# A fused attention and mixture-of-experts block: one matmul more in each of seven products and two fewer in each plain one, second-layer weights loaded twice by tiles, eight query tiles to a head

## The chip, the cores and the metric
One Trainium2 chip; the kernel runs on one core of it, in one launch. The metric is the device time of an execution in microseconds (us), the median of several runs.

## The reference
2048 tokens x of width D = 448. The output is the sum of x, of an attention block (16 heads of 28) and of a mixture of 8 experts, both on the normalised x. All 8 experts are chosen for each token (K = 8), so every expert runs on every token and is weighted by a softmax over its logits. Everything is float32.

```python
xn = _layernorm(x)
# attention: qkv = xn @ wqkv; 16 heads of 28; softmax(q k^T * 28**-0.5) v; @ wo
# experts, w1: 8 x 448 x 1792, w2: 8 x 1792 x 448
for e in range(8):
    h = _silu(xn @ w1[e]) @ w2[e]
    out = out + w[e] * h          # w: softmax of xn @ w_gate
return x + attention + out
```

## The kernel before
**Precision.** TensorE works in float16. Each float32 operand is split into a high and a low float16 part, and a product takes three matmuls: high by high, high by low, low by high.

**First layer.** The 1792 hidden columns of an expert go in groups of 5, 5 and 4 tiles of 128 (`GROUPS`, 24 in all), the tokens in 4 chunks of 512 (`C`). A unit (`unit`, line 1073) is one group on one chunk. D = 448 is cut into blocks of 128, 128, 128 and 64. For four of a group's tiles, two pairs, the first two blocks of D go through a seven-product scheme (Strassen-Winograd: products of sums of weight blocks with sums of x blocks, `strassen`, line 1084, 256 tokens wide, 6 matmuls each over the two pairs), and the third block and the 64 rows left over are added by `plain` (line 1098, 8 matmuls each) and `tails` (line 1111). In a group of five the fifth tile is done directly (`single`, line 1153). The sums of weights are made for each pair in `split_w1` (line 542), into buffers `wa` (seven blocks, high and low) and `wc` (third block and rest); the sums of x in `sums_of_x` (line 1173). These are split, transposed by DMA, stored in DRAM (`xd`) and loaded again for each unit (`sums_x`, line 1225, tile `xt`).

**Second layer.** `summed` (line 1295) multiplies silu's outputs (`hh`, `hl`, made by `silu`, line 1241: tanh on ScalarE, a product on VectorE, high part on ScalarE, low part on GpSimd) with the group's second-layer weights and adds the result to `acc` on VectorE. It is put between the products of the next unit (`tick`). `load_group` (line 470) loads a group's weights `r1` and `r2` whole; `scale_w2` (line 510) finds their largest absolute value with two reductions, `split_w2` (line 624) scales and splits one tile of `r2` at a time.

**Attention.** `attention` (line 1369) goes over tiles of 128 queries, four at a time (`NB`) for a head; K, Q and V of the head are loaded for each four. Scores go to a double bank (line 1420), their extreme is found on VectorE (line 1424), the exponential on ScalarE (line 1437), its high part on ScalarE (line 1445) and its low part on VectorE (line 1440); both parts are transposed by DMA (line 1458) and multiplied with V (lines 1492, 1499). After four heads the output projection follows (`project`).

**Order of work.** No order is written out by hand. Each function adds jobs with an engine, an estimated duration, a due time v, and the buffers read and written. `Plan.run` (line 103) simulates the engines when the program is built and emits, for each engine, the job with the smallest v whose inputs and buffers are there. Buffers with one tag are a ring: they are given out in the order in which they were created, and the next one waits until one is free. The order is fixed in the program then, and each engine's queue and SP's (which issues the DMAs) runs strictly in it. First-layer and second-layer work and attention are interleaved this way from about 125 us on; before, the projections of x run (`phase0`, line 655). `phase0`'s tiles are in a pool of their own, whose room attention takes when its last job is issued.

## Time and profile before

| | |
|---|---|
| median of 3 runs | 2608.8 us (2608.79 to 2611.23) |
| the profiled execution | 2610.42 us, its span 2608.6 us |
| TensorE (PE) busy | 2572.0 us, 20863 matmuls |
| VectorE (DVE) busy | 2328.2 us |
| ScalarE (ACT) busy | 2065.4 us |
| GpSimd (POOL) busy | 1370.4 us |
| DMA queue of SP | 463 MB, 83.7% of 16 engines' span |
| granted TensorE clock | 0.999 |

The span goes from the first to the last instruction of the profiled execution. PE's busy time is the union of overlapping matmuls, so a mean duration is longer than what a matmul adds to the stream. PEld is the weight load, which overlaps. SPq is SP's queue of DMA issues.

### The profile page before, as it was taken

How to read it: one execution, taken by the hardware profiler on the slowest of the kernel's cores; microseconds unless marked ns; L12 is line 12 of the kernel's file. 1: busy time of each engine (PE TensorE's matmuls, PEld its weight loads, DVE VectorE, ACT ScalarE, POOL GpSimd, SP SyncE). 2: the span in 40 equal slices, each digit the busy share in tenths (PEclk: the TensorE clock that was granted, in tenths of full speed). 3: DMA queues.
4: the chain of work that ended last, by engine and by line, in shares of the span. 5: the costliest groups of instructions: out<-in, count | busy, mean ns of one | idle time of the engine just before them, and what ended most of it. 6: DMA issues, size and time to landing. Idle time of an engine off the chain costs nothing.

```text
span 2608.6 us, 54466 instructions
## 1 busy us (share of the span) xinstructions
PE 2572.0 (99%) x20863; PEld 1612.0 (62%) x20863; DVE 2328.2 (89%) x3127; ACT 2065.4 (79%) x2993; POOL 1370.4 (53%) x1377
## 2 busy tenths in 40 slices
PE   9999999999999999999999999999999999999999
PEld 4466666666666666666665666666666666666666
DVE  9689899988998899988999899898889889998986
ACT  5578878886887888778788888888788887878874
POOL 2365545563655545456455556456455653645633
PEclk9999999999999999999999999999999999999999
DMA  9868979887898899968898888877888888997875
GB/s 264 206 153 167 185 173 189 180 174 168 171 195 172 178 175 202 182 155 178 189 182 179 166 189 187 168 177 177 174 177 190 168 172 180 187 197 162 181 157 136
DMA packets 1262757, 466.94 MB, mean 179 GB/s; under 512 B 1169440, under 2 KB 1218080, under 8 KB 1262496
## 3 DMA queue, kind: packets, MB, share of 16 engines
q1 hardware_dynamic: 1261936, 463.44, 83.7%
q8 instruction: 164, 2.69, 0.5%
q14 instruction: 97, 0.79, 0.1%
q10 hardware_dynamic: 560, 0.02, 0.0%
HBM read 160.09 MB, written 17.35 MB: 68 GB/s over the span
## 4 chain that ended last, share of the span: by engine, by line
PE 73%; DVE 14%; ACT 8%; issue 3%; DMA 3%; SPq 0%; DVEq 0%; ACTq 0%
PE banks L1311 29%; PE banks L1090 13%; PE banks L1106 10%; PE banks L1420 7%; PE banks L1162 5%; DVE mx L1424 4%; DVE pl L1440 3%; PE banks L1499 3%; PE banks L1492 2%; ACT pf L1437 2%; ACT ph L1445 2%; DMA tl<-pl 2%; DVE t L1249 2%; PE banks L1117 2%; DVE acc L1322 1%
## 5 line engine op out<-in xcount | busy, mean ns | idle before, releaser
L1311 PE MATMUL banks<-w,hr 128*128 128x448 f16 x5364 | 1083.2, 353 | 2.1 <-DVE t L1249 1.1
L1255 POOL TENSOR_TENSOR hr<-t,hr 128x512 f16<-128x512 f32 x448 | 606.7, 1368 | 576.6 <-ACT hr L1253 553.0
L1437 ACT ACTIVATE pf<-banks,mx 128x1024 f32<-128x1024 f32 x512 | 568.9, 1111 | 322.6 <-DVE mx L1424 316.9
L1311 PEld LDWEIGHTS <-hr 128*128 128x128 f16 x5364 | 516.3, 98 | 493.2 <-issue 24.0
L1440 DVE SCALAR_TENSOR_TENSOR pl<-pf,ph 128x1024 f16<-128x1024 f32 x512 | 718.2, 1404 | 57.2 <-ACT ph L1445 56.6
L1424 DVE TENSOR_REDUCE mx<-banks 128x1 f32<-128x1024 f32 x512 | 622.4, 1216 | 77.0 <-PE banks L1420 60.3
L1445 ACT ACTIVATE ph<-pf 128x1024 f16<-128x1024 f32 x512 | 539.8, 1055 | 6.2
L1090 PEld LDWEIGHTS <-wa 128*128 128x128 f16 x4032 | 392.4, 98 | 115.9 <-issue 13.7
L1106 PE MATMUL banks<-xs,wc 128*128 128x256 f16 x3072 | 395.2, 272 | 1.0 <-DVE banks L1141 0.7
L1106 PEld LDWEIGHTS <-wc 128*128 128x128 f16 x3072 | 299.3, 98 | 61.7 <-issue 5.0
L1246 ACT ACTIVATE t<-banks,the 128x512 f32<-128x512 f32 x448 | 289.8, 683 | 54.2 <-PE banks L1117 38.7
L1249 DVE SCALAR_TENSOR_TENSOR t<-t,banks 128x512 f32<-128x512 f32 x448 | 291.6, 678 | 36.7 <-ACT t L1246 35.7
L1090 PE MATMUL banks<-xt,wa 128*128 128x256 f16 x2304 | 314.4, 272 | 5.4 <-ACT banks L1131 4.7
L1420 PE MATMUL banks<-K,Q 112*128 112x512 f16 x1024 | 306.3, 380 | 2.8 <-ACT pf L1437 2.6
L1253 ACT ACTIVATE hr<-t 128x512 f16<-128x512 f32 x448 | 267.5, 627 | 18.6 <-DVE t L1249 17.9
L1322 DVE SCALAR_TENSOR_TENSOR acc<-banks,gwe,acc 128x448 f32<-128x448 f32 x383 | 254.7, 674 | 30.5 <-PE banks L1311 29.9
L1090 PE MATMUL banks<-xs,wa 128*128 128x256 f16 x1728 | 235.8, 272 | 0.4 <-DVE acc L1322 0.4
L567 POOL TENSOR_TENSOR wc<-r,wc 128x512 f16<-128x512 f32 x64 | 83.6, 1306 | 208.1 <-ACT wc L563 186.0
L634 POOL TENSOR_TENSOR w<-r,w 128x448 f16<-128x448 f32 x112 | 138.5, 1240 | 100.8 <-ACT w L631 94.7
L1162 PE MATMUL banks<-xs,wc 128*128 128x512 f16 x704 | 164.5, 379 | 1.2 <-DVE t L1249 1.2
L1420 PEld LDWEIGHTS <-Q 112*128 112x128 f16 x1024 | 94.4, 98 | 77.3 <-issue 20.8
L1499 PEld LDWEIGHTS <-th 128*128 128x128 f16 x4096 | 118.6, 96 | 13.9 <-issue 4.7
(174 smaller groups left out, 2343.0 us busy)
## 6 DMA issues: line engine op xcount, KB each, us to landing
xt<-xd SPq DMA_DIRECT2D x71, 512.0 KB
K<-qk SPq DMA_DIRECT2D x512, 56.0 KB
r<-in_B_w_dram SPq DMA_DIRECT2D x16, 1120.0 KB
V<-vs SPq DMA_DIRECT2D x64, 256.0 KB
r<-in_B_w_dram SPq DMA_DIRECT2D x16, 960.0 KB
Q<-qk SPq DMA_DIRECT2D x256, 28.0 KB
r<-in_B_w_dram SPq DMA_DIRECT2D x8, 896.0 KB
r<-in_B_w_dram SPq DMA_DIRECT2D x8, 768.0 KB
```

What stands on the lines that cost most here:

```text
L1090: nc.tensor.matmul(bank()[:, q * HC : (q + 1) * HC], w, xx, start=(start and q == 0 and i == 0), stop=True, skip_group_check=True,)
L1106: nc.tensor.matmul(bank()[:, q * HC : (q + 1) * HC], ww, xx, start=False, stop=True, skip_group_check=True,)
L1162: nc.tensor.matmul(z(), rows[:, blk, :], xx, start=(i == 0), stop=(i == NTERM - 1))
L1246: add("ACT", 686, lambda: nc.scalar.activation(t(), z(), AF.Tanh, scale=th_()[:, 0:1]), v, r=[z, (th_, 0)], w=[t])
L1249: lambda: nc.vector.scalar_tensor_tensor(t(), t(), 1.0, z(), op0=ALU.add, op1=ALU.mult),
L1255: add("POOL", 1159, lambda: nc.gpsimd.tensor_tensor(hl(), t(), hh(), ALU.subtract), v, r=[t, hh], w=[hl])
L1311: nc.tensor.matmul(y()[:, 0:D], a, wv, start=(i == 0 and u == 0), stop=(i == g - 1 and u == 2))
L1420: nc.tensor.matmul(b()[:, cs], q()[:, q0 : q0 + P], k()[:, cs], start=True, stop=True)
L1424: nc.vector.tensor_reduce(m()[:, n, j : j + 1], b(), op=ALU.min, axis=AX.X)
L1437: nc.scalar.activation(p(), s(), AF.Exp, bias=m()[:, n, j : j + 1], scale=-1.0)
L1440: nc.vector.scalar_tensor_tensor(l()[:, js], p(), P_SCALE, h()[:, js], op0=ALU.mult, op1=ALU.subtract)
L1445: add("ACT", 1060, lambda: nc.scalar.activation(h()[:, js], p(), AF.Copy, scale=P_SCALE), v, r=[p], w=[(h, j)])
```

## The change
It does these things:
- `plain` keeps the matmuls of the third block's high part with x's high part and of the 64 left over; the two with a low part (weights high by x low, weights low by x high) leave it. Each of the seven products gets one matmul more per half instead, a mixed one: a block of the third part's weights (`crossed`, four new 128x128 blocks behind the `wa` tile, or a block of `wc`) by a block of the third part of x or a sum of such blocks, scaled by `LAMBDA`.
- `split_w1` makes the four new blocks for each pair: one ScalarE copy (`less`), four GpSimd operations (`crosses`, `more_crosses`). The single tile's `wc` goes into a ring of its own, `wz`, of one buffer.
- `sums_of_x` makes the sums of the third block for each chunk on VectorE (`first_two`, `last_two`); x's sums are 6 blocks in each of two half tiles `xt` (3 buffers in place of 2 whole ones of 8 blocks), transposed, stored and loaded by halves. At the start the second half of the second chunk's sums lies in a buffer of the ring `wa`.
- second-layer weights are loaded by tiles of 128x448 into a ring of two buffers, once for the largest value (`scale_w2`, one reduction per tile) and once more for the split.
- `s5` moves into the ring `th` of silu's intermediate; `u`, `ro` and `ohl` of attention share one buffer (`uo`); `wo` in `phase0` is loaded into two buffers of the query and key weights.
- attention takes eight query tiles to a head: K and V are loaded once for eight, the output buffer `ost` holds eight.

```diff
-NB, TL, TH = 4, 1, 4
-RWA, RWC, RW2, RH, RHC, RT, RPP, RPF = 4, 4, 7, 8, 2, 3, 2, 2
+NB, NH, TL, TH = 4, 8, 1, 4
+RWA, RWC, RWZ, RW2, RH, RT, RPF, RR = 4, 4, 1, 7, 8, 3, 2, 2
+LAMBDA = 2048.0
...
+    def tile_of_w2(gi, j, name, v):
+        e, f0, _ = GROUPS[gi]
+        b = buf("mp", [P, D], F32, f"r2{name}{gi}_{j}", tag="r2", bufs=RR)
+        dma(lambda: b(), lambda: w2[e, (f0 + j) * P : (f0 + j + 1) * P, :], v, w=[b], kb=224, rate=3.6)
+        return b
...
     def scale_w2(gi, v):
...
+        for j in range(g):
+            r2 = tile_of_w2(gi, j, "m", v)
+            add("DVE", 600, lambda j=j, r2=r2: abs_max(m5()[:, j : j + 1], r2(), AX.X), v, r=[r2], w=[(m5, j)])
+        def most_of_all():
+            for i, (j0, j1) in enumerate(((0, 2), (2, g))):
+                nc.vector.tensor_reduce(m2()[:, i : i + 1], m5()[:, j0:j1], op=ALU.max, axis=AX.X)
...
-        wa = buf("mp", [P, 2, 7 * P], F16, f"wa{gi}_{j}", tag="wa", bufs=RWA)
+        wa = buf("mp", [P, 18 * P], F16, f"wa{gi}_{j}", tag="wa", bufs=RWA)
...
+        def less():
+            nc.scalar.activation(
+                r(2, 3), wc()[:, 0 : 2 * P].rearrange("p (k c) -> p k c", k=1), AF.Copy, scale=1 / LAMBDA
+            )
+        def crosses():
+            a11, a21 = r(2, 3, 0, 1)[:, 0], r(2, 3, 1, 2)[:, 0]
+            nc.gpsimd.tensor_tensor(crossed(3), a21, of_wc(1, 1), ALU.add)
+            nc.gpsimd.tensor_tensor(crossed(1), a11, a21, ALU.subtract)
+        def more_crosses():
+            a11 = r(2, 3, 0, 1)[:, 0]
+            nc.gpsimd.tensor_tensor(crossed(0), crossed(3), a11, ALU.subtract)
+            nc.gpsimd.tensor_tensor(crossed(2), of_wc(1, 0), crossed(0), ALU.subtract)
...
     def split_w2(gi, j, v):
         w = buf("mp", [P, 2, D], F16, f"w2_{gi}_{j}", tag="w2", bufs=RW2)
-        so, r2 = SC[gi][1], R[gi][1]
+        so, r2 = SC[gi][1], tile_of_w2(gi, j, "s", v)
...
-            s5 = buf("mp", [P, C], F32, f"s5{name}", tag="s5")
+            s5 = buf("mp", [P, C], F32, f"s5{name}", tag="th", bufs=RT)
...
-                        for i, (w, xx) in enumerate(((h, xp[0]), (h, xp[1]), (l, xp[0]))):
+                        for i, (w, xx) in enumerate(((h, xp[0]), (h, xp[1]), (l, xp[0]), (wx, xx3))):
...
-                        for ww, xx in (
-                            (w[:, 0, 0], xs[:, 2, t[i]]), (w[:, 0, 0], xs[:, 6, t[i]]), (w[:, 1, 0], xs[:, 2, t[i]]),
-                            (w[:, 0, 1], xs[:, 3, t[i]]),
-                        ):
+                        for ww, xx in ((w[:, 0, 0], xs[:, 2, t[i]]), (w[:, 0, 1], xs[:, 3, t[i]])):
...
+            def first_two():
+                t1, t2 = pair(0)
+                nc.vector.tensor_tensor(t1, b12, b11, ALU.subtract)
+                nc.vector.scalar_tensor_tensor(t2, t1, -LAMBDA, b22, op0=ALU.mult, op1=ALU.add)
+            def last_two():
+                t1, t2, t3, t4 = *pair(0), *pair(1)
+                nc.vector.scalar_tensor_tensor(t3, b12, -LAMBDA, b22, op0=ALU.mult, op1=ALU.add)
+                nc.vector.tensor_tensor(t4, b21, t2, ALU.subtract)
+                nc.vector.tensor_scalar(t1, t1, LAMBDA, None, op0=ALU.mult)
...
         def sums_x(gi, b, v):
-            XS_[gi, b] = x = buf("mp", [P, 8, HC], F16, f"xt{gi}_{b}", tag="xt", bufs=2)
+            first = not gi and b < 2
+            own = 3 - 2 * b if first else 2
+            xt = [buf("mp", [P, 6, HC], F16, f"xt{gi}_{b}_{q}", tag="xt", bufs=3) if q < own else None for q in range(2)]
+            XS_[gi, b] = [x or buf("mp", [P, 18 * P], F16, f"xw{b}_{q}", tag="wa", bufs=RWA) for q, x in enumerate(xt)]
...
-        TILES = [(4 * k + a, t0 + n) for k in range(H // 4) for t0 in range(0, NT, NB) for a in range(4) for n in range(NB)]
+        TILES = [(4 * k + a, t0 + n) for k in range(H // 4) for t0 in range(0, NT, NH) for a in range(4) for n in range(NH)]
...
             if i % NB == 0:
-                load_k(i, 0, at(i - 2) if i else at(-9))
-                load_k(i, 1, at(i - 1))
-                load_v(i, at(i - 2))
+                if i % NH == 0:
+                    load_k(i, 0, at(i - 2) if i else at(-9))
+                    load_k(i, 1, at(i - 1))
+                    load_v(i, at(i - 2))
```

## Rows read from the trace of the kernel before

**Rows 1.** The table of engines: busy time, share of the span, instructions.
```profile
PE 2572.0 (99%) x20863; PEld 1612.0 (62%) x20863; DVE 2328.2 (89%) x3127; ACT 2065.4 (79%) x2993; POOL 1370.4 (53%) x1377
```

**Rows 2.** Busy time of each engine in two windows: PE, PEld, DVE, ACT, POOL (with instructions), granted clock, DMA share, GB/s.
```profile
0.00:130.00 130.00, 121.84 (x592) 57.99 (x593) 103.17 (x262) 74.43 (x146) 39.66 (x50) 1.00 0.91 235
130.00:2543.00 2413.00, 2388.68 (x19727) 1514.39 (x19725) 2182.61 (x2808) 1959.74 (x2801) 1307.55 (x1303) 1.00 0.85 177
```

**Rows 3.** The waits of PE: us in total, times, longest us.
```profile
PE banks L1492 <- DMA tl<-pl: 6.5, 7, 2.1
PE banks L1090 <- ACT banks L1131: 4.7, 6, 1.3
```

**Rows 4.** PE's groups of matmuls, shapes apart: count, busy us and mean ns of one, idle time before.
```profile
L1106 PE MATMUL banks<-xs,wc 128*128 128x256 f16 x3072 | 395.2, 272 | 1.0 <-DVE banks L1141 0.7 <-DVE the L505 0.3
L1090 PE MATMUL banks<-xt,wa 128*128 128x256 f16 x2304 | 314.4, 272 | 5.4 <-ACT banks L1131 4.7 <-DVE banks L1137 0.2
L1090 PE MATMUL banks<-xs,wa 128*128 128x256 f16 x1728 | 235.8, 272 | 0.4 <-DVE acc L1322 0.4
```

**Rows 5.** The chain of waits between 1200 and 1260 us: start, us, what.
```profile
1210.56 0.87 PE banks L1106 x8
...
1221.24 0.54 PE banks L1117 x8
...
1232.98 1.31 PE banks L1090 x12
```

**Rows 6.** DVE's groups, shapes apart: count, busy us and mean ns of one, idle time before.
```profile
L1440 DVE SCALAR_TENSOR_TENSOR pl<-pf,ph 128x1024 f16<-128x1024 f32 x512 | 718.2, 1404 | 57.2 <-ACT ph L1445 56.6
...
L412 DVE TENSOR_REDUCE mb<-r 128x1 f32<-128x896 f32 x32 | 34.2, 1074 | 2.2 <-DMA r<-in_B_w_dram 2.2
L412 DVE TENSOR_REDUCE mb<-r 128x1 f32<-128x1344 f32 x16 | 24.7, 1543 | 1.2 <-DMA r<-in_B_w_dram 1.2
...
L1481 DVE TENSOR_REDUCE top<-mx 128x4 f32<-128x8 f32 x64 | 9.6, 150 | 0.2
L1183 DVE TENSOR_SCALAR xa<-acc,rstd,shift 128x256 f32<-128x256 f32 x16 | 7.3, 492 | 0.1
```

**Rows 7.** Line 412's reductions of a 128x448 and a 128x896 f32 tile, listed by line: duration ns min/median/max (the 603 is that of the 128x448 ones).
```profile
L412 DVE TENSOR_REDUCE mkq<-rqk x5: 603/1067/1068, 12.1 to 20.8; 128x1 f32<-128x896 f32 x3, 128x1 f32<-128x448 f32 x2
```

**Rows 8.** ACT's group of 128x256 copies in the split of first-layer weights.
```profile
L586 ACT ACTIVATE wa<-r 128x256 f16<-128x256 f32 x48 | 19.2, 400 | 0.0
```

**Rows 9.** The costliest and the cheapest of POOL's groups of 128x128 f32 operations on first-layer weights.
```profile
L598 POOL TENSOR_TENSOR r<-r 128x128 f32<-128x128 f32 x48 | 35.1, 732 | 3.8
...
L597 POOL TENSOR_TENSOR r<-r 128x128 f32<-128x128 f32 x48 | 24.7, 515 | 2.1
```

**Rows 10.** Line 1440 listed by line: duration ns min/median/max, first and last start.
```profile
L1440 DVE SCALAR_TENSOR_TENSOR pl<-pf,ph x512: 1205/1224/3096, 142.0 to 2572.4; 128x1024 f16<-128x1024 f32 x171
```

**Rows 11.** The DMA queue of SP (packets, MB, share of 16 engines), and issues with their sizes.
```profile
q1 hardware_dynamic: 1261936, 463.44, 83.7%
...
xt<-xd SPq DMA_DIRECT2D x71, 512.0 KB
K<-qk SPq DMA_DIRECT2D x512, 56.0 KB
...
V<-vs SPq DMA_DIRECT2D x64, 256.0 KB
```

**Rows 12.** SP's time to issue a DMA on line 388: ns min/median/max.
```profile
L388 SPq DMA_DIRECT2D K<-qk x512: 313/383/1988, 130.5 to 2531.1; - x171
...
L388 SPq DMA_DIRECT2D r<-in_B_w_dram x96: 383/526/2395, 10.6 to 2427.8; - x96
```

**Rows 13.** The timeline of PE from 124 to 138 us: start, us, line; the end of the first unit and the start of the second.
```profile
135.38 0.61 PE L1117 MATMUL banks<-xs,wc 64*128 64x256 f16 x8
...
137.03 0.82 PE L1090 MATMUL banks<-xt,wa 128*128 128x256 f16 x6
```

**Rows 14.** The timelines of PE, ACT, POOL, SP and DVE about the end of one group (1281 to 1303 us): the last second-layer products with the old weights and the first with the new, the split of two tiles between, the load of the weights of the group after, their first reduction.
```profile
1283.48 1.87 PE L1311 MATMUL banks<-w,hr 128*128 128x448 f16 x9
...
1296.66 1.31 PE L1311 MATMUL banks<-w,hr 128*128 128x448 f16 x6
...
1283.42 0.65 ACT L630 ACTIVATE r<-r,scob 128x448 f32<-128x448 f32 x1
...
1284.75 2.20 POOL L634 TENSOR_TENSOR w<-r,w 128x448 f16<-128x448 f32 x2 [0.91 <-ACT w L631]
...
1286.98 0.41 SPq L388 DMA_DIRECT2D r<-in_B_w_dram  x1
...
1295.90 1.54 DVE L412 TENSOR_REDUCE mb<-r 128x1 f32<-128x1344 f32 x1
```

**Rows 15.** The timeline of SP's queue: the transposes of the sums of chunks 2 and 3 into two `wa` buffers.
```profile
105.47 2.89 SPq L1213 DMA_TRANSPOSE xw<-xt  x1
...
124.96 1.26 SPq L1213 DMA_TRANSPOSE xw<-xt  x1
```

**Rows 16.** The timeline of PE: the first product of the fourth unit.
```profile
189.78 0.82 PE L1090 MATMUL banks<-xs,wa 128*128 128x256 f16 x6
```

**Rows 17.** The waits of DVE: us in total, times, longest us.
```profile
DVE mx L1424 <- PE banks L1420: 60.3, 70, 3.7
DVE pl L1440 <- ACT ph L1445: 56.6, 74, 2.3
```

More of the change, by code (lines that the diff above doesn't have):

```diff
@@ L618, in split_w1 @@
         add("ACT", 630, high, v, r=keys, w=[(wc, 0)])
-        add("POOL", 1303, low, v, r=[*keys, (wc, 0)], w=[(wc, 1)])
+        add("POOL", 1303, low, v, r=[*keys, *third, (wc, 0)], w=[(wc, 1)])
         add("ACT", 630, high_sums, v, r=ab, w=[(wa, 2)])
         add("POOL", 1377, low_sums, v, r=[*ab, (wa, 2)], w=[(wa, 3)])
+        add("ACT", 420, less, v, r=[(wc, 0)], w=third)
+        add("POOL", 1150, crosses, v, r=[(wc, 1), *third], w=[(wa, 4)], steps=2)
+        add("POOL", 1150, more_crosses, v, r=[(wc, 1), *third], w=[(wa, 4)], steps=2)
         W1[gi, j] = wa, wc
@@ L633, in low @@
         def low():
[L634 to L637 removed]
+            nc.gpsimd.tensor_tensor(w()[:, 1, :], r2(), w()[:, 0, :], ALU.subtract)
+        add("ACT", 1265, high, v, r=[so], w=[r2, (w, 0)])
+        add("POOL", 1038, low, v, r=[r2, (w, 0)], w=[(w, 1)])
         W2[gi, j] = w
@@ L1171, in single, with blocks, sums_of_x @@
             return lastz
-        def sums_of_x(c, x, v):
+        def blocks(b):
+            return b() if len(b.shape) == 3 else b()[:, 0 : 6 * HC].rearrange("p (k c) -> p k c", k=6)
+        def sums_of_x(c, xt, v):
+            far = [q for q in range(2) if not xt[q]]
+            xws = []
             for j in range(2):
@@ new lines, in last_two @@
+            def last_two():
[3 more added lines that the diff above has]
+                nc.vector.tensor_scalar(t1, t1, LAMBDA, None, op0=ALU.mult)
+            outs = [(xws[0], "third", q) if q in far else (xt[q], 2) for q in range(2)]
+            add("DVE", 560, first_two, v, r=xkeys(c), w=outs[:1], port=138)
+            add("DVE", 760, last_two, v, r=xkeys(c), w=outs, port=600)
@@ L1223, in sums_of_x @@
+            for q in range(2):
+                dma(
+                    lambda q=q: xd[c, q, :, 4:6],
+                    lambda q=q: xws[0]()[:, 8 * P + 2 * q * HC : 8 * P + 2 * (q + 1) * HC].rearrange("p (k c) -> p k c", k=2)
+                    if q in far else blocks(xt[q])[:, 4:6],
+                    v, r=[outs[q]], w=[("xd", c, q, 2)], kb=128,
                 )
         def sums_x(gi, b, v):
-            XS_[gi, b] = x = buf("mp", [P, 8, HC], F16, f"xt{gi}_{b}", tag="xt", bufs=2)
-            if not gi and b < 2:
-                sums_of_x(b, x, v)
+            first = not gi and b < 2
```

182 lines of the change are left out of this document (103 added, 79 removed).

## The prediction

> **What bounds the kernel now.** I read the table of engines first: TensorE (PE) is busy 2572.0 us of a span of 2608.6 us, VectorE (DVE) 2328.2, ScalarE (ACT) 2065.4, GpSimd (POOL) 1370.4 [rows 1]. Then two windows, to see where PE is not busy: 8.2 us of the first 130 and 24.3 of the 2413 in the middle, which leaves some 4 of its 36.6 idle us for the last 65, at a granted clock of 1.00, the 2.4 GHz level [rows 2]. Then PE's list of waits: its largest entries are 6.5 us over seven waits for a DMA and 4.7 over six for ACT [rows 3]. So the kernel is bound by the number of PE columns, and nothing else is a constant brake; DVE at 2182.6 of 2413 us (90%) in the middle is the next engine. Last I read the price of a matmul from the chain of waits, not from its duration: one 128x256 matmul "takes" 272 ns, but eight in a row advance the chain by 0.87 us and twelve by 1.31 us, 109 ns each [rows 4, 5].
>
> **PE work removed and added.** A unit (one chunk of 512 tokens in one group of weights; 24 groups x 4 chunks = 96 units) issues 42 matmuls in the seven products and 32 in the four plain ones; the counts 4032 and 3072 are 96 times that [rows 4]. After the change each product has one more matmul per half (+14), and each plain one keeps 2 of 4 (-16): 5376 and 1536, two fewer per unit, 192 fewer in all. Shape, type and bank halves are the same, and every matmul has its own weight load before and after. 192 x 109 ns = **21.0 us less**. If a pair went at the share of PE's busy time that falls on it, 129 to 137 ns a matmul [rows 4], it would be 26 us; I take 21, the pitch in an undisturbed row. All other PE work stays.
>
> **DVE.** The two reductions over a group's second-layer weights (34.2 + 24.7 us in all) become one per tile, 112 at 603 ns (a 128x448 reduction) = 67.5, and two tiny ones per group, 48 x 150 ns = 7.2: +15.8 us [rows 6, 7]. The sums of the third block of x are 5 operations of 128x256 for each of 4 chunks; the nearest row is the 492 ns of a 256-wide f32 one [rows 6], which makes 10 us; with operands of half the size it may be half of that, and I take the row. Together +26 us, 2354.
>
> **ACT.** One 128x256 copy per pair of weight tiles, 48 x 400 ns = +19.2 us [rows 8]: 2085 of some 2590, still 80%. It is covered: ACT's 540 us of idle time hold it. Uncovered it would be those 19 us.
>
> **POOL.** Four 128x128 operations per pair of tiles, 192; the lines that do such operations average 515 to 732 ns [rows 9]: 99 to 141 us, and I take the middle, +120. POOL is idle 1238 us, and a group's weights are split during the group before, so the time itself is hidden. What it does to DVE isn't: the subtraction on line 1440, which reads two SBUF tiles, has a median of 1224 ns and a mean of 1404 [rows 6, 10]; 512 x 180 ns = 92 us are lost beside 1370 us of POOL, 0.067 us for each. 120 x 0.067 = +8 us of DVE; bounds 0 and 120 (every microsecond blocks DVE). I take the measured share. DVE is then 2362 us.
> The Trainium skill (SBUF — State Buffer, Who interferes with whom) states that such a DVE instruction and a GpSimd one that reads SBUF exclude each other for a whole instruction; at its worst, each new POOL operation on the other's time, DVE would gain the 120 us of the upper bound. The trace agrees that they disturb each other, but shows a fifteenth of that.
>
> **DMAs and SP's queue.** K goes from 512 loads of 56 KB to 256, V from 64 of 256 KB to 32: -23 MB. The second-layer weights come twice (+25.7 MB; 24 loads become 224 tiles of 224 KB), and the sums of x as 142 loads of 384 KB in place of 71 of 512 (+18.6 MB); with 1 MB more of stores the sum is +22 MB [rows 11]. At the 235 GB/s of the first 130 us with the engines 91% busy [rows 2] that is 85 us of all engines: the queue's 83.7% becomes 87 to 88%. Issuing: -256 x 0.383 - 32 x 0.38 + 200 x 0.383 to 0.526 + 71 x 0.38, so -7 to +22 us on SP [rows 12]: 1% of its time, nothing. SP is behind in order: a load of a tile waits there until a reduction or a split frees one of two buffers, and the transposes of the probabilities queue behind it. Against that, half of the loads of K go, which wait there for the scores that free their buffers.
>
> **Buffers.** Halving the loads of K and V, the larger output buffer and the shared "uo" buffer cost PE nothing: they move only when tiles are loaded. The sum held in "th" now takes one of silu's three buffers, in turn after the last of the unit before. Usually more than 11 us lie between a unit's tails (1221.24) and the next unit's second product (1232.98) [rows 5]; at the tightest place 1.65 us do (135.38 to 137.03) [rows 13]. I price it at 0 to 5 us.
> Second-layer weights at a group's end: at 1285.3 PE ends the last product with the old ones, at 1296.66 begins the first with the new: 11.3 us, in which it does the next unit's products [rows 14]. In this time tile 2 must be split (2.4 us, from 1283.42 to half of the POOL pair), which frees the buffer for tile 4, and tile 4 must land and be split (2.4 us). A landing of up to 6.5 us is hidden; the 1.1 MB load issued at 1286.98 was being reduced at 1295.90, 8.9 us, and a fifth of the bytes should take less [rows 14]. Cost 0; at the 8.9 us it is 2.4 us at each of the 8 boundaries between groups of five, 19 us.
> At the start, the sums of chunks 2 and 3 go through one "wa" buffer in place of two, since the second chunk keeps one. A buffer turned over in 19.5 us (105.47 to 124.96) [rows 15]; four turns reach 105 + 4 x 19.5 = 183, and chunk 3 is wanted by the unit that begins at 189.8 [rows 16]. It just fits; 0 to 12 us, I take 2.
>
> **Sum.** PE is idle 24.3 us in the middle because feeders are late now and then. DVE's idle share there falls from 9.5% to about 7.6% (2182.6 + 26 in 2392 us); if late arrivals grow as that share shrinks, x 1.25, that is +6; fewer waits at K's buffers give some back: +3, and +2 at the start. 2608.6 - 21 + 5 = 2592.6 of span. The profiled execution took 2610.42, 1.8 above its span, and the median of the runs is 2608.8, 1.6 below it; so 2594.4 for such an execution and **2593 us** for the median.
>
> **Rivals.**
> (1) DVE takes over as the bound: slower. If its 280 us of idle time are waits for an order that doesn't shrink, the span is 2362 + 280 = 2642 us. It decides from the point where DVE gives up less than 33 of its 280 us. For it: DVE waits 56.6 us for ACT's copy on line 1445, which gets no faster; against it: 60.3 us are waits for PE's scores, and PE has less to do [rows 17]. Chance 0.10.
> (2) The gain is there and waits take it: tile 4 late at each boundary between groups of five (19), the start (5): 2608.8 - 21 + 24 = 2612. For it, the thin slack at a boundary (6.5 us against at most 8.9) and at the start (183 against 189.8); against it, PE has attention work to put in. Chance 0.17.
> (3) Small loads are slow ones and fill the DMA engines. The queue is busy 83.7% of the span, 2183 us; with the 85 us above, 340 us stay free. At the rate used above a tile of 229 kB takes 0.89 us of all engines [rows 2]; it decides from the point where each of the 224 takes 1.5 us more. At 2.6 us a tile the queue alone needs 2183 + 85 + 224 x 1.7 = 2650 us. Chance 0.03.
> The Trainium skill (DMA: Bandwidth & Descriptors, Measured) advises loads of 1 MiB or more, and its fit of 2.0 us plus bytes over 436 GB/s gives 2.5 us for a tile, an estimate, which would all but bring this rival about; the window's rate, reached by loads in flight together, speaks against adding up the fixed part.
> (4) The change does not do what it says: the matmuls are two fewer, but the mixed ones advance 112 ns each in place of 109, which undoes the gain (6912 x 3 ns = 21 us); 2609. Nothing in the rows speaks for it. Chance 0.03.
> The forecast keeps 0.67.
>
> **Range and chances.** A change of under 0.2%, 5.2 us, is about what a measurement of this kernel can't tell from none (three runs lie 2.4 us apart). Faster than 2603.6: nearly all of the forecast and a little of (2), 0.69; within 0.2%: most of (2), (4), the worst of the forecast, 0.15; slower: (1), (3), the rest of (2), 0.16. The low end is the 26 us of the busy shares with no new wait, 2583, rounded to 2584; the high end 2614 is where (2) ends, and leaves (1) and (3) out.
>
> **What would show it.** Right: 5376 and 1536 matmuls in the two lines, PE's busy time down by 21 us, its idle time in the middle 24 to 35 us, DVE near 2360. Wrong: PE idle over 50 us with DVE or the reduction of a tile named as releaser (1); gaps before the second-layer products at every second or third group's end, with a weight load as releaser (2); PE waiting over 20 us for the transposed probabilities (3); eight matmuls in over 0.88 us (4).

## The result and the profile after

The changed kernel takes 2624.7 us (median of four runs, 2620.7 to 2626.8); the kernel before, on the same chip, 2609.95. The ratio is 1.0053 [1.0040, 1.0066]: slower by 0.5%, where 2593 us (2584 to 2614) and a gain of 0.6% were predicted. The profiled execution took 2626.82 us with a span of 2625.0, 16.4 us above that of before.

The table of engines of the kernel after, and the DMA queue of SP (answers to [rows 1, 11]):

```profile
PE 2562.2 (98%) x20671; PEld 1595.8 (61%) x20671; DVE 2349.4 (90%) x3261; ACT 2074.7 (79%) x3041; POOL 1475.5 (56%) x1569
...
q1 hardware_dynamic: 1275888, 485.73, 87.8%
```

PE has its 192 matmuls fewer, but is busy only 9.8 us less, and idle for 62.8 us (2625.0 - 2562.2) where it was idle for 36.6. The missing 11 us of the 21 are matmuls at a lower clock: the records have 27 us at the 1.2 GHz level beside 3 before, in five stretches that each begin during or just after waits of PE of 2 to 3 us (those before 136.35, 147.89, 602.26, 911.52 and 1021.99 us). So 26.2 of idle time plus 11 of clock minus 21 of work is the 16 us. Two windows of the kernel after (columns as in [rows 2]) say where:

```profile
0.00:130.00 130.00, 123.65 (x603) 59.23 (x604) 107.44 (x280) 74.38 (x147) 44.22 (x59) 1.00 0.90 236
130.00:2543.00 2413.00, 2359.44 (x19449) 1484.77 (x19447) 2207.84 (x2927) 1974.72 (x2851) 1407.74 (x1486) 0.99 0.90 187
```

The middle is idle for 53.6 us in place of 24.3, with the DMA engines at 0.90 in place of 0.85. Its first 35 us alone, after and then before, in the same columns:

```profile
130.00:165.00 35.00, 24.00 (x141) 14.07 (x139) 25.58 (x38) 21.55 (x28) 5.74 (x5) 0.80 0.89 197
```
```profile
130.00:165.00 35.00, 33.55 (x239) 21.94 (x237) 29.69 (x43) 30.13 (x46) 23.67 (x24) 1.00 0.67 155
```

Here PE works 9.6 us less than before, and at a granted clock of 0.80. The other 20 us of idle time that the middle has gained lie behind this stretch. The timelines of ACT, DVE and PE in this stretch of the kernel after (start, us, what, idle time before it and its releaser; answers to [rows 13]):

```profile
129.63 0.60 ACT L1172 ACTIVATE s<-banks 128x512 f32<-128x512 f32 x1 [1.33 <-POOL xt L1246]
135.03 0.69 ACT L1330 ACTIVATE t<-banks,the 128x512 f32<-128x512 f32 x1 [4.80 <-DVE banks L1180]
...
131.88 0.62 DVE L413 TENSOR_REDUCE mb<-r2m 128x1 f32<-128x448 f32 x1 [4.25 <-DMA r2m<-in_B_w_dram]
...
133.16 1.03 PE L1133 MATMUL banks<-xt,wa 128*128 128x256 f16 x8 [2.60 <-DVE banks L1176]
136.35 1.01 PE L1504 MATMUL banks<-K,Q 112*128 112x512 f16 x2 [2.15 <-DMA K<-qk]
...
147.89 1.01 PE L1504 MATMUL banks<-K,Q 112*128 112x512 f16 x2 [2.94 <-ACT pf L1521]
151.19 1.44 PE L1201 MATMUL banks<-xs,wc 128*128 128x512 f16 x3 [2.29 <-DVE t L1333]
```

DVE stands 4.25 us at a reduction whose tile has not landed. The addition on line 1176, which is behind it in DVE's order, then lets PE go on at 133.16, and through line 1180 the tanh waits on ACT. One landing stops three engines, because each works in order. It isn't the only late one: the next wait of PE, before 136.35, is for a tile of K, and the chain of waits there passes over that landing:

```profile
127.85 6.94 DMA K<-qk
```

A reduction's tile is late again further on: DVE and PE about 905 us, and the chain of waits there.

```profile
902.58 0.67 DVE L1406 SCALAR_TENSOR_TENSOR acc<-banks,gwe,acc 128x448 f32<-128x448 f32 x1
907.44 0.62 DVE L413 TENSOR_REDUCE mb<-r2m 128x1 f32<-128x448 f32 x1 [4.18 <-DMA r2m<-in_B_w_dram]
...
911.52 1.01 PE L1504 MATMUL banks<-K,Q 112*128 112x512 f16 x2 [3.09 <-ACT pf L1521]
```
```profile
901.42 5.99 DMA r2m<-in_B_w_dram
```

PE's line names ACT; the chain goes back from there through two DVE operations to the reduction and its tile. The lists of waits of the kernel after, for PE, DVE and ACT (answers to [rows 3, 17]; a wait is put down to the last link only):

```profile
PE banks L1504 <- ACT pf L1521: 19.3, 21, 3.1
PE banks L1576 <- DMA tl<-pl: 6.7, 6, 3.2
PE banks L1133 <- DVE banks L1176: 4.5, 6, 2.6
...
DVE mb L413 <- DMA r2m<-in_B_w_dram: 9.6, 6, 4.3
DVE scbb L438 <- DMA scmb<-mxs: 4.0, 5, 2.1
...
ACT r2s L660 <- DMA r2s<-in_B_w_dram: 3.6, 1, 3.6
```

PE's groups of matmuls, and two pieces of its chain of waits near 1337 us (answers to [rows 4, 5]):

```profile
L1133 PE MATMUL banks<-xs,wa 128*128 128x256 f16 x1920 | 279.3, 274 | 0.0
L1145 PE MATMUL banks<-xs,wc 128*128 128x256 f16 x1536 | 225.8, 273 | 2.8 <-DVE banks L1180 1.7 <-DVE top L1565 1.1
L1395 PE MATMUL banks<-w,hr 128*128 128x448 f16 x5364 | 1083.6, 353 | 2.9 <-DVE t L1333 1.5 <-DMA Q<-qk 0.6 <-DVE u L1601 0.4
...
1337.32 0.88 PE banks L1133 x8
1338.19 0.44 PE banks L1145 x4
```

The pitch is 109 to 110 ns, mixed matmuls included, and no second-layer product waits for a split tile. Last, the new operations on POOL and ACT, and the lines of the subtraction and of the reductions with their duration in ns, min/median/max (answers to [rows 7 to 10]):

```profile
L636 POOL TENSOR_TENSOR wa<-wa,r 128x128 f16<-128x128 f16 x48 | 34.6, 720 | 0.0
L632 POOL TENSOR_TENSOR wa<-r 128x128 f16<-128x128 f32 x48 | 27.8, 579 | 0.0
L637 POOL TENSOR_TENSOR wa<-wc,wa 128x128 f16<-128x128 f16 x48 | 25.1, 522 | 3.8
L631 POOL TENSOR_TENSOR wa<-r,wc 128x128 f16<-128x128 f32 x48 | 24.8, 517 | 18.5 <-ACT r L625 18.1
...
L625 ACT ACTIVATE r<-wc 128x256 f32<-128x256 f16 x48 | 19.8, 412 | 1.6 <-POOL wc L572 1.6
...
L1524 DVE SCALAR_TENSOR_TENSOR pl<-pf,ph x512: 1205/1226/5930, 143.1 to 2542.6; 128x1024 f16<-128x1024 f32 x171
...
L413 DVE TENSOR_REDUCE mb<-r2m x112: 601/607/621, 68.3 to 2486.3; 128x1 f32<-128x448 f32 x112
```

### The profile page after: what moved, and what is told of

Same layout as the page of the kernel before. It is cut to its first block, busy times and chain, and to the rows that moved or that the text cites. A ratio compares the mean times of both kernels' runs of the same rounds, so it can differ in the third digit from the quotient of the medians.

```text
span 2625.0 us, 54530 instructions
## 1 busy us (share of the span) xinstructions
PE 2562.2 (98%) x20671; PEld 1595.8 (61%) x20671; DVE 2349.4 (90%) x3261; ACT 2074.7 (79%) x3041; POOL 1475.5 (56%) x1569
## 3 DMA queue, kind: packets, MB, share of 16 engines
q1 hardware_dynamic: 1275888, 485.73, 87.8%
## 4 chain that ended last, share of the span: by engine, by line
PE 68%; DVE 16%; ACT 7%; DMA 5%; issue 3%; POOL 1%; SPq 0%; DVEq 0%; ACTq 0%; POOLq 0%
PE banks L1395 27%; PE banks L1133 16%; PE banks L1504 6%; PE banks L1145 5%; DVE pl L1524 4%; PE banks L1201 4%; DVE mx L1508 4%; PE banks L1583 3%; ACT pf L1521 2%; PE banks L1576 2%; DVE t L1333 2%; PE banks L1156 2%; PE banks L962 1%; ACT ph L1529 1%; DVE acc L1406 1%
## 5 line engine op out<-in xcount | busy, mean ns | idle before, releaser
L1339 POOL TENSOR_TENSOR hr<-t,hr 128x512 f16<-128x512 f32 x448 | 594.6, 1341 | 584.0 <-ACT hr L1337 541.8
L1524 DVE SCALAR_TENSOR_TENSOR pl<-pf,ph 128x1024 f16<-128x1024 f32 x512 | 729.7, 1427 | 39.8 <-ACT ph L1529 37.5
L1508 DVE TENSOR_REDUCE mx<-banks 128x1 f32<-128x1024 f32 x512 | 622.8, 1216 | 62.6 <-PE banks L1504 54.6
L1133 PEld LDWEIGHTS <-wa 128*128 128x128 f16 x4800 | 468.0, 98 | 130.3 <-issue 16.7
L1133 PE MATMUL banks<-xt,wa 128*128 128x256 f16 x2866 | 384.9, 272 | 8.6 <-DVE banks L1176 4.5
L1504 PE MATMUL banks<-K,Q 112*128 112x512 f16 x1024 | 308.4, 382 | 21.8 <-ACT pf L1521 19.3
L1133 PE MATMUL banks<-xs,wa 128*128 128x256 f16 x1920 | 279.3, 274 | 0.0
L1145 PE MATMUL banks<-xs,wc 128*128 128x256 f16 x1536 | 225.8, 273 | 2.8 <-DVE banks L1180 1.7
L664 POOL TENSOR_TENSOR w<-r2s,w 128x448 f16<-128x448 f32 x112 | 136.4, 1220 | 155.4 <-ACT w L661 144.1
L1145 PEld LDWEIGHTS <-wc 128*128 128x128 f16 x1536 | 149.2, 98 | 46.4 <-issue 7.8
```

The costliest lines, as they stand in the source:

```text
L1133: nc.tensor.matmul(bank()[:, q * HC : (q + 1) * HC], w, xx, start=(start and q == 0 and i == 0), stop=True, skip_group_check=True,)
L1145: nc.tensor.matmul(bank()[:, q * HC : (q + 1) * HC], ww, xx, start=False, stop=True, skip_group_check=True,)
L1339: add("POOL", 1159, lambda: nc.gpsimd.tensor_tensor(hl(), t(), hh(), ALU.subtract), v, r=[t, hh], w=[hl])
L1504: nc.tensor.matmul(b()[:, cs], q()[:, q0 : q0 + P], k()[:, cs], start=True, stop=True)
L1508: nc.vector.tensor_reduce(m()[:, n, j : j + 1], b(), op=ALU.min, axis=AX.X)
L1524: nc.vector.scalar_tensor_tensor(l()[:, js], p(), P_SCALE, h()[:, js], op0=ALU.mult, op1=ALU.subtract)
```

## The experiments

Two kinds are to be kept apart. In e1 to e5 and e9 every engine keeps the order of the kernel that was edited; in the others the planner makes a new order. Two runs change nothing but the order: e17 that of before (+0.3%), e12 that of after (+0.6%). All ratios are to the kernel before on the same chip; "idle" is the span less PE's busy time of the profiled execution, "130 to 195" PE's busy us there and the granted clock.

| kernel | us | ratio | PE idle | DMA queue | 130 to 195 |
|---|---|---|---|---|---|
| before | 2602 to 2611 | 1 | 36.6 | 83.7% | 63.6, 1.00 |
| after | 2624.7 | 1.0053 [1.0040, 1.0066] | 62.8 | 87.8% | 54.0, 0.89 |
| e1 before, fewer matmuls | 2597.1 | 0.9965 [0.9952, 0.9978] | 41.2 | 82.5% | 63.0, 1.00 |
| e18 the same, new order | 2596.6 | 0.9971 [0.9959, 0.9983] | 38.2 | 83.0% | 62.9, 1.00 |
| e17 before, new order | 2612.7 | 1.0027 [1.0015, 1.0039] | 36.0 | 82.1% | 61.2, 0.95 |
| e4 before, load twice | 2710.0 | 1.0405 [1.0389, 1.0420] | 104.6 | 81.9% | 59.6, 0.95 |
| e10 before, eight query tiles | 2597.3 | 0.9967 [0.9953, 0.9981] | 25.0 | 78.8% | 63.2, 1.00 |
| e6 before, tiles | 2691.5 | 1.0327 [1.0312, 1.0343] | 98.1 | 89.2% | 62.9, 1.00 |
| e9 e6, small first loads | 2670.5 | 1.0248 [1.0232, 1.0264] | 87.1 | 87.0% | 62.6, 1.00 |
| e13 e6, five buffers | 2707.7 | 1.0396 [1.0380, 1.0411] | 108.3 | 89.8% | 57.6, 0.92 |
| e11 tiles and eight query tiles | 2656.1 | 1.0198 [1.0182, 1.0215] | 68.7 | 87.5% | 62.3, 1.00 |
| e2 after, memsets | 2612.5 | 1.0028 [1.0016, 1.0039] | 52.8 | 86.6% | 53.9, 0.89 |
| e3 after, small first loads | 2605.5 | 0.9997 [0.9988, 1.0007] | 45.8 | 83.2% | 56.2, 0.89 |
| e5 e2 and e3 | 2605.9 | 1.0000 [0.9990, 1.0009] | 46.8 | 83.6% | 56.6, 0.89 |
| e12 after, later landing planned | 2633.6 | 1.0109 [1.0091, 1.0127] | 63.1 | 85.2% | 52.4, 0.92 |
| e7 after, four query tiles | 2638.0 | 1.0128 [1.0114, 1.0143] | 66.9 | 88.5% | 54.1, 0.92 |
| e8 e7, own s5 | 2650.7 | 1.0173 [1.0159, 1.0187] | 77.3 | 89.5% | 56.0, 0.95 |
| e14 after, three tile buffers | 2636.0 | 1.0127 [1.0112, 1.0142] | 70.4 | 86.0% | 43.8, 0.79 |
| e15 e7, own chunk sums, six split tiles (2 runs) | 2694.9 | 1.0348 [1.0327, 1.0369] | 109.1 | 87.7% | 55.2, 0.89 |
| e16 e7, no tiles, five split tiles | 2738.1 | 1.0509 [1.0485, 1.0532] | 144.4 | 88.4% | 41.1, 0.84 |

`Plan.run` also leaves the span that it simulated when it made the order (`self.span`), a figure of the program and not of the chip. It is 2589 us for before, 2571 for after, 2583 for e6, 2584 for e11, 2580 for e13, 2591 for e17 and 2584 for e12. So after's order promises 18 us of the 21, and the order of tiles alone is 6 us shorter than before's, though it runs 85 us longer: what these kernels lose comes from work or landings that take longer than the planner assumes, not from a longer order. e15's and e16's orders, 2605 and 2600 us, are longer by themselves.

**e1: before, 192 matmuls fewer.** In the plain scheme's loop:

```diff
-                        ):
+                        )[: 3 if f and i else 4]:
```

> The kernel before, in its own order, without the last matmul of one plain product (the 64-row block's high part, in both halves): 192 matmuls of 128x256 less, nothing else changed; the output lacks that part. If PE's columns set the pace (the prediction's first term), the time falls by 21 us, to 2589, and PE's idle time stays near 37 us. If the order's other engines set the pace in places, PE's idle time grows and the time falls by less: by 10 us if half of it turns into waits, by nothing if DVE is the bound.

0.35% less, 9 us of the 21. The profiled spans, from different chips, show PE's busy time down by 17.9 and 4.6 more of idle time, 13 us; the interval of the ratio allows 6 to 12.5. So part of the removed work comes back as waiting even where nothing is added.

**e2: after, mixed blocks as memsets.**

```diff
-            nc.gpsimd.tensor_tensor(crossed(3), a21, of_wc(1, 1), ALU.add)
-            nc.gpsimd.tensor_tensor(crossed(1), a11, a21, ALU.subtract)
+            nc.gpsimd.memset(wa()[:, 14 * P : 16 * P], 0.0)
...
-            nc.gpsimd.tensor_tensor(crossed(0), crossed(3), a11, ALU.subtract)
-            nc.gpsimd.tensor_tensor(crossed(2), of_wc(1, 0), crossed(0), ALU.subtract)
+            nc.gpsimd.memset(wa()[:, 16 * P : 18 * P], 0.0)
```

> The changed kernel in its own order, with the four GpSimd operations per pair of tiles that make the mixed blocks replaced by two fills with zero (128x256 each), which read nothing; the mixed products are zero. Theory 'GpSimd blocks VectorE' (single subtractions on VectorE took up to 5.9 us beside GpSimd): POOL's busy time falls by 70 to 100 us, the mean of the subtraction on VectorE falls from 1427 to about 1390 ns, the longest ones vanish, and the time falls by 5 to 15 us. Theory 'late landings': no more than 3 us. Theory 'start': PE busy in 130 to 195 us stays at 54 of 65.

POOL's busy time falls by 80 us and the whole by 0.25%, 6.5 us. The stall at 130 us stays. But the theory that GpSimd blocks VectorE isn't shown by it: the subtraction's mean goes from 1427 to 1424 ns only, where 1390 was expected, and its longest stays at 5.9 us. By what the 6.5 us come is open.

```profile
L1520 DVE SCALAR_TENSOR_TENSOR pl<-pf,ph 128x1024 f16<-128x1024 f32 x512 | 728.4, 1424 | 35.2 <-ACT ph L1525 33.1 <-DMA tl<-pl 1.6
```

**e3: after, small first loads.** The reduction reads 64 loaded columns seven times.

```diff
-        dma(lambda: b(), lambda: w2[e, (f0 + j) * P : (f0 + j + 1) * P, :], v, ...)
+        n = 64 if name == "m" else D
+        dma(lambda: b()[:, 0:n], lambda: w2[e, (f0 + j) * P : (f0 + j + 1) * P, 0:n], v, ...)
```

> The changed kernel in its own order; the first load of each second-layer weight tile, for the largest value, brings 64 of 448 columns, and the reduction reads these 64 seven times, so VectorE works as long as before; the scale comes from a seventh of the weights. 22 MB less by DMA, and each of these loads lands sooner. Theory 'late landings' (VectorE waits in order for such a load, 9.6 us in all, and PE after it): that wait falls below 2 us, the DMA queue's share from 87.8 to about 84%, PE's idle time from 63 to 50 us or less, the time by 8 to 15 us. Theories 'GpSimd blocks VectorE' and 'start': under 4 us.

The loss is gone: 0.56%, 15 us, for 22 MB, with all operations in place. The waits of DVE for first tiles fall from 9.6 to 4.0 us (below 2 was expected), those of PE for `tl` from 6.7 to 2.4. A shorter load is both fewer bytes on the queue and an earlier landing of its own; this run doesn't part the two.

```profile
DVE mb L413 <- DMA r2m<-in_B_w_dram: 4.0, 3, 3.1
PE banks L1577 <- DMA tl<-pl: 2.4, 1, 2.4
```

**e4: before, each group's load of w2 issued twice.**

```diff
+        def twice():
+            for _ in range(2):
+                nc.sync.dma_start(r2()[:, 0:g, :], w2[e, cs, :].rearrange("(f p) d -> p f d", p=P))
```

> The kernel before in its own order, each group's second-layer weights loaded twice by the same whole load (24 more DMAs, 25.7 MB): the change's traffic without its small tiles, its two buffers and its new waits. If DMA traffic itself costs time (transposes land later): DMA share 83.7 to 88%, PE's waits for the transposed probabilities from 6.5 to over 15 us, time up by 8 us or more. If only waits for particular loads cost: time within 3 us of before.

105 us for 25.7 MB. The list of waits of DVE:

```profile
DVE mb L412 <- DMA r<-in_B_w_dram: 45.5, 14, 6.3
```

The DMA engines are not full (81.9%); the reduction, placed for one load, stands in DVE's order until both have landed. The Trainium skill (DMA: Bandwidth & Descriptors, Measured) advises loads of 1 MiB or more. No run here tests size alone: these loads of 0.9 and 1.1 MB stand in an order made for loading once, the tiles of e6 (85 us for the same bytes) in an order made for tiles.

**e5: e2 and e3 together.** Both diffs above.

> The kernel after in its own order of work, with both earlier cuts at once: the first loads of w2's tiles bring 64 of 448 columns (the reductions read those seven times), and the four mixed blocks of a pair of hidden tiles are two memsets on POOL instead of four tensor operations. It leaves out most of the maxima of w2 and the mixed blocks' values. Alone the small loads gave 0.56 % (0.9997 in place of 1.0053) and the memsets 0.25 % (1.0028). Theory A (transfers and the port shared by DVE and POOL cost separately, and the start's jam of some 10 us stays): the gains add, 0.9972 of before, about 2598 us, with the first 65 us after 130 still at 54 to 56 us of TensorE work. Theory B (both cuts take away the same late DVE operations): the gains don't add, about 0.9995, 2604 us. If the removed matmuls paid in full and nothing else was left, it would be 0.992, 2585 us.

They don't add: 1.0000 beside 0.9997, theory B in its number. Mixed blocks and late tiles don't cost separately.

**e6: before, w2 by tiles, twice.** Buffers, reductions and split as in the change's diff (`tile_of_w2`, `scale_w2`, `split_w2`), all else as before.

```diff
-        r2 = buf("mp", [P, GMAX, D], F32, f"r2_{gi}", tag="r2")
+        b = buf("mp", [P, D], F32, f"r2{name}{gi}_{j}", tag="r2", bufs=RR)
...
-        so, r2 = SC[gi][1], R[gi][1]
+        so, r2 = SC[gi][1], tile_of_w2(gi, j, "s", v)
```

> The kernel before with one part of the change alone: w2 comes by tiles of 128x448 in two buffers, once for the maxima and once for the split, in place of one load of a group; mixed products, query tiles and the chunk sums stay as before, and its order of work is planned anew. Theory A (the second load costs time by lateness): 10 to 18 us slower than before, ratio 1.004 to 1.007, with DVE's reductions waiting for tiles (some 10 us) and transposed probabilities late. Theory B (the second load is hidden where POOL's mixed blocks and the shared buffers are absent): within 0.2 % of before.

85 us, about five times the 10 to 18 that theory A expected. The waits of PE, DVE and ACT:

```profile
PE banks L1496 <- DMA tl<-pl: 29.7, 23, 3.0
PE banks L1424 <- ACT pf L1441: 14.9, 20, 2.2
...
DVE mb L412 <- DMA r2m<-in_B_w_dram: 24.7, 14, 5.2
DVE scba L437 <- DMA scma<-mxs: 4.8, 4, 1.6
DVE scbb L437 <- DMA scmb<-mxs: 4.3, 5, 1.3
...
ACT r2s L634 <- DMA r2s<-in_B_w_dram: 10.5, 5, 2.8
```

DVE and ACT stand 44 us at landings of second-layer weights and of scales (the last four lines), and PE then at what the two make: `pf`, and `pl` through its transpose.

**e9: e6's order, small first loads** (the diff of e3).

> The kernel of the run with tiles alone, in its own order of work, with the first loads of w2's tiles cut from 448 to 64 columns (the reductions read those seven times; most of the maxima are left out). Theory A (the time follows the bytes that the DMA engines have to carry: tiles alone had 492.7 MB, 89.2 % of the engines' time and 2691 us): with 470.6 MB the share falls to some 84 % and the time to 2605 to 2615 us. Theory B (not the bytes but the order: the split waits for a second landing, tiles come in two buffers, and the plan was made with shorter landings): the time stays above 2660 us with tl<-pl still ending 20 us or more of TensorE's idle time.

Some 20 us of the 85 go with the bytes of the first loads, as the 15 in e3; 65 do not: theory B, though `tl` costs PE no less than with full loads. Its waits:

```profile
PE banks L1497 <- DMA tl<-pl: 30.7, 26, 2.9
...
DVE mb L412 <- DMA r2m<-in_B_w_dram: 15.9, 9, 4.2
...
ACT r2s L635 <- DMA r2s<-in_B_w_dram: 7.3, 4, 2.8
```

**e13: e6 with five buffers for tiles.** Planned anew.

```diff
-RWA, RWC, RW2, RH, RHC, RT, RPP, RPF, RR = 4, 4, 7, 8, 2, 3, 2, 2, 2
+RWA, RWC, RW2, RH, RHC, RT, RPP, RPF, RR = 4, 4, 7, 8, 2, 3, 2, 2, 5
```

> The kernel before with w2 by tiles loaded twice (2691 us), with five buffers for the tiles in place of two, so that a tile's load needn't wait for a reduction or a split to free one; bytes are the same. Theory A (two buffers: a load stands in SP's queue until one is free, lands late, and what follows it in SP's and DVE's order is late too): the 65 us that aren't bytes mostly go, 2620 to 2640 us. Theory B (the number of separate DVE operations and landings, whatever the buffers): 2670 us or more.

Theory B: five buffers don't help. The splits no longer wait for tiles, but the waits only move to the scales:

```profile
DVE scba L437 <- DMA scma<-mxs: 20.5, 9, 4.3
DVE scbb L437 <- DMA scmb<-mxs: 17.3, 9, 4.1
...
DVE mb L412 <- DMA r2m<-in_B_w_dram: 12.8, 10, 2.2
```

**e10: before, eight query tiles.** As in the change; loads of K and V under

```diff
+                if i % NH == 0:
```

> The kernel before with another part of the change alone: eight query tiles to a head, so that K and V are loaded half as often (23 MB less); weights in one load of a group, no mixed products. Theory A (bytes are what costs beyond some 84 % of the DMA engines' time, and before stands below it): little to gain, 2597 to 2606 us, DMA share 79 to 80 %. Theory B (before too loses its 20 to 30 us of idle time to late transfers): 2585 to 2595 us.

Faster than both kernels, 0.9967, with 23 MB less (theory A, at its fast end); the waits of DVE and ACT for weights and scales are down to 0.2 us.

**e11: tiles and eight query tiles, no mixed products** (e6 and e10).

> The kernel before with two parts of the change, w2 by tiles loaded twice and eight query tiles, without the mixed products. Bytes are as before's within 4 MB. Theory A (bytes): 2605 to 2620 us, DMA share 84 to 85 %, so the 85 us of tiles alone are given back. Theory B (order and lateness of the tiles): 2660 us or more.

Bytes as before, yet 50 us slower, just short of theory B. Its engines, and what waits:

```profile
PE 2585.3 (97%) x20863; PEld 1615.0 (61%) x20863; DVE 2344.7 (88%) x3239; ACT 2064.1 (78%) x2993; POOL 1379.1 (52%) x1377
...
PE banks L1424 <- ACT pf L1441: 17.1, 22, 3.8
PE banks L1496 <- DMA tl<-pl: 14.0, 8, 2.7
...
ACT r2s L634 <- DMA r2s<-in_B_w_dram: 10.4, 6, 3.9
```

From here the kernel after differs by the mixed products and the sums of x: PE's busy time falls by 23.1 us, its idle time by 5.9, the ratio by 0.0145. That is 38 us, more than the 21 that the removed matmuls can give, so the order or the other buffers have a share in it; with 7 and 15 us for an order alone (e17, e12) the part of the matmuls can't be told from this. **What it does show: the tiles cost time in e11 already, without a mixed product.**

**e12: after, a tile planned to land 5.5 us after its issue.**

```diff
-        dma(..., kb=224, rate=3.6)
+        dma(..., kb=224, rate=3.6, land=5500)
```

> The kernel after with one number of its planner changed: a tile of w2 is taken to land 5.5 us after its issue, so that the operations that read it are given later places in the engines' orders. Nothing is computed otherwise. Theory A (DVE's reduction stands in order in front of operations that could run, so lateness turns into TensorE's idle time): the waits of the reduction on its tile (9.6 us) go below 4 us, and the time falls by 5 to 15 us, 2610 to 2620 us. Theory B (the DMA engines are full; whoever is asked later waits instead, transposes above all): the reduction's waits go, tl<-pl or pf waits of TensorE grow by as much, and the time stays within 5 us of after.

The reduction's waits on its tiles go, `pf` costs PE 30.2 in place of 19.3, and the time is 0.56% longer by the ratios: theory B in kind, at more than its price. (The profiled execution, 2623.8 us, is the fastest of the four; the others took 2633 to 2635.) The stall at the start stays, 52.4 us of work: the chain there still begins at the landing of a tile (4.83 us from 126.57) and now comes by way of POOL and a copy on ACT to the same addition on line 1176, 2 us later than in the kernel after. A later place for the reduction moves the wait and doesn't end it.

```profile
PE banks L1504 <- ACT pf L1521: 30.2, 27, 4.0
...
134.45 0.70 DVE L1176 TENSOR_TENSOR banks<-banks,s 128x512 f32<-128x512 f32 x1 [7.33 <-ACT s L1172]
```

**e7 and e8: after with four query tiles; then s5 with its own buffer.**

```diff
-NB, NH, TL, TH = 4, 8, 1, 4
+NB, NH, TL, TH = 4, 4, 1, 4
...
-            s5 = buf("mp", [P, C], F32, f"s5{name}", tag="th", bufs=RT)
+            s5 = buf("mp", [P, C], F32, f"s5{name}", tag="s5")
```

> The kernel after with four query tiles to a head in place of eight: keys and values are loaded for each four, and the outputs' buffers are half as large. It frees room, which the next kernel uses; by itself it is the base for that one. More transfers of K and V than in the kernel after, so not faster than it: 1.005 to 1.010 of before, and the stall at 130 to 160 us as after (TensorE 54 us busy of the 65 from 130 to 195, granted clock 0.89).

> The kernel of the run before this one (after, four query tiles) with one line changed back: the copy s5 of a product's bank has a buffer of its own again and doesn't take its turn among the three of the chunk sums. Theory A (s5 behind the sums of chunk 2 and 3, which wait for the one buffer of split weights, makes the stall at 130 to 160 us): the 65 us from 130 have 60 to 65 us of TensorE work at a clock near 1.00, and the time falls by 8 to 12 us against the kernel with four query tiles. Theory B (the stall is made by w2's tile loads that land late there, DVE waiting in order for them): the window stays below 57 us with a clock of 0.9, and the time falls by under 4 us.

Four tiles cost 0.75%, more than expected. An own s5 gives 2 us of work in the window and a longer whole: s5's turn in "th" is not the stall.

**e14: after, three buffers for raw tiles, six for split ones.**

```diff
-RWA, RWC, RWZ, RW2, RH, RT, RPF, RR = 4, 4, 1, 7, 8, 3, 2, 2
+RWA, RWC, RWZ, RW2, RH, RT, RPF, RR = 4, 4, 1, 6, 8, 3, 2, 3
```

> The kernel after with three buffers for the raw tiles of w2 in place of two, paid for by one buffer of split tiles (six in place of seven). Theory A (two buffers are what makes tiles late): 2600 to 2615 us. Theory B (they aren't, or the split tiles' buffers matter as much): within 8 us of after or slower.

Theory B, as e13; the stretch from 130 to 195 gets worse, 43.8 us of work at 0.79. **e15: the second chunk's sums in buffers of their own** (with four query tiles, six split tiles):

```diff
-            own = 3 - 2 * b if first else 2
-            ... tag="xt", bufs=3)
+            own = 2
+            ... tag="xt", bufs=4)
```

> The kernel after with four query tiles and six buffers of split tiles (to make room), and with one thing of the change undone: the second chunk's sums of x have two buffers of their own (four in all) and hold no buffer of split weights. Read is only the stretch from 130 to 195 us. Theory A (the chunk sums that wait for the one free buffer of split weights make the stall): 60 to 63 us of TensorE work there, clock 1.00. Theory B (the stall comes from the number of operations on DVE, ACT and POOL at the start): 54 to 57 us, clock about 0.9. The whole time will be slower than after, by K's and V's loads and fewer buffers.

55.2 us at 0.89: theory B's figures, in two runs. They don't settle it: this kernel has six split tiles, as e14 has, whose stall is the deeper one, and no run has the six alone. **e16: after with one load of w2 for a group** (four query tiles; `RW2` 5 in place of 7):

> The kernel after with one thing of the change undone: w2 comes once, in one load of a group, as before. To make room, four query tiles and five buffers of split tiles in place of seven. Mixed products and chunk sums as after. Theory A (tiles are the loss, the rest gains): 2590 to 2605 us in spite of the fewer buffers. Theory B (the mixed products' own work on DVE, POOL and ACT takes the gain): 2615 us or more.

2738 us, in theory B's range but not by its reason. Five buffers of split tiles and the 23 MB for K and V change too much with it, and it says nothing of tiles.

**e17 and e18: controls of the order.** Before with a landing planned later, and e1 planned anew:

```diff
-M_AT, A_AT, LEAD, END, LAND, TURN = 60.0, 0.0, 130.0, 2585.0, 3500, 4500
+M_AT, A_AT, LEAD, END, LAND, TURN = 60.0, 0.0, 130.0, 2585.0, 4000, 4500
...
-                return product, 8 * H_NS, ...
+                return product, (6 if f and i else 8) * H_NS, ...
```

> The kernel before with exactly its work, and one number of its planner changed: transfers are taken to land 4.0 us after they begin in place of 3.5, which gives every engine another order. Theory A (an order costs some 10 us more or less): 2600 to 2620 us, and differences of 50 us and more between other kernels are their edits'. Theory B (the orders of before and after are each a good find, and any new plan is far off): 2640 us or more, and then what kernels planned anew show of an edit is worth little beside the runs in an order that was kept.

> The kernel before with 192 of the plain scheme's matmuls left out, as in the first experiment (2597 us there, in the old order), and the order planned anew with that. Theory A (the removed columns turn into time once the other engines' work is placed closer): 2585 to 2592 us. Theory B (they turn into idle time, since other engines and transfers set the pace too): 2597 to 2610 us. Theory C (a new plan is worse by itself): 2620 us or more.

This other order costs 7 us and that of e12 15, so differences of 50 us are hardly an order's; those of 10 to 15 between planned kernels (e8, e14) only say that nothing was won. The cut of matmuls gives 8 us in a new order, too, where theory A expected the whole gain and the planned span is 21 us shorter: theory B, at its fast end.

## Why the prediction was wrong

**The step that failed is "DMAs and SP's queue".** It gave the second load bytes and issue time ("1% of its time, nothing") and no price for landing late, and "Sum" allowed 5 us for all new waits; PE's idle time grew by 26. The bytes, the 87 to 88% and the counts came as predicted; that this is free did not. I summed up the engines' free time and found 340 us to spare; what counts, by the chains of waits, is when one transfer lands. The second load put 112 reductions on DVE and 112 scalings on ACT that each need a fresh landing, on two engines that work in order and also make the probabilities. Shown: the first loads' bytes and their landings are 15 us in the order of after (e3) and 20 in that of e6 (e9); tiles without mixed products are slower by 85 us, or by 50 with eight query tiles (e6, e11). I had priced the reductions by their duration alone (+15.8 us, hidden; 66.5 us measured beside the 67.5 I took) and a late tile only at the ends of groups, where the "Cost 0" held: no wait for one came. That the loss goes by landings on in-order engines is read from the chains of waits and is not shown by an experiment of its own: e12 takes the reductions' waits away, and others come in their place.

**PE's work** was right in its counts and pitch; rival (4) is out. Of the 21 us, the cut alone gives 8 to 9 (e1, e18), as waits grow: this term was too large by some 12, of the 32 us between forecast and result. What it gives on top of tiles and eight query tiles can't be told from the 38 us between e11 and after.

**The start** was mis-sized: 2 us predicted; lost were 9.6 of idle time and a clock of 0.80 over 35 us. The tile that DVE waits for at 131.88 is one link; with the reduction placed later the same addition waits as long by way of POOL and ACT (e12). e6, e9 and e11 have tiles and no stall (62.3 to 62.9 us), so tiles alone needn't make one; e13, without a mixed product, has a smaller one (57.6 us at 0.92), so the mixed part isn't the only way to it. Undoing s5's place (e8) or POOL's blocks (e2) doesn't end it, and e15 leaves the chunk sums' buffer open. The sums of the third blocks and ACT's `less` were not tried alone.

**DVE, ACT and POOL** came out near: 2349 for 2362, 2075 for 2085, +105 for +120 us. Line 1524's mean rose by 23 ns, 12 us in all for the 8 predicted; one took 5.93 us. That nearness is luck: with 80 us of POOL's new work gone the mean falls by 3 ns (e2), 1.5 us in all, so POOL's new operations aren't what made the rise, and the 0.067 us of the prediction isn't their price. The Trainium skill (SBUF — State Buffer, Who interferes with whom) has a DVE operation with two SBUF inputs and a POOL operation that reads SBUF contend; e2's 3 ns are all that these runs show of it.

**Rivals.** Rival (1)'s sign was half there (over 50 us of idle time; PE's largest releaser is ACT's `pf`, with tile reductions behind it in the chain above), but DVE is no bound: it is idle for 276 us of the span (2625.0 - 2349.4), and what counts is where it stands, not how long it works. Rival (2), 2612, had the right direction: the start did cost, group ends nothing (2.9 us of waits on line 1395, none for a tile). Rival (3) asked the right resource, but its mechanism, a queue too full to end in time, isn't what the queue's 87.8% shows.

**Open:** what the 65 us of tiles are that stay with small first loads. Five buffers in place of two don't help (e13), and the order is not longer by the planner's own account; the waits for landings on DVE and ACT are what grows with it (6.1 us before, 0.2 in e10, 19.6 after, 18.9 in e11, 36 in e9, 48 in e6, 58 in e13, each the sum of the waits for weights and scales), but they are fewer us than the time lost, and e12 and e14 have only 11 and 12 and are no faster than after.

## What to carry to other kernels

Where an in-order engine that feeds the bound must wait for a landing, price the landing's lateness there, and not only the bytes against the queue's free share: free share is an average, and the 12 to 16% of it here hid 20 MB badly. A second read of data from memory to save a buffer is a new dependence on each engine that reads it; try that part alone first. And keep the order fixed when testing a small edit, or run controls with another order to know what an order is worth (7 and 15 us here). Where the program plans its own order, compare its planned span with the measured one as well: it tells a worse order from an order that the chip doesn't keep.

## What the runs showed of the hardware

Much the same 22 to 26 MB had very different prices, though they are not the same loads and only e3's and e4's pairs keep one order: 9 us where the queue was at 79 to 84% (e10 against before), 15 at 83 to 88% (e3 against after), 35 at 87.5 to 89% (e11 against e6), 105 where one reduction waited for a doubled load at 82% (e4). And PE's idle time can cost twice: stretches at 1.2 GHz followed its waits, 27 us in the kernel after, some 11 us of longer matmuls, while its mean granted clock of 0.995 against 0.999 hardly shows it. It isn't in proportion: e9 is idle for 87 us at a mean clock of 0.997.
